# A kernel with a recorded issue order: warm-up in three parts, first tile first on both queues, stores in groups of 6, 6 and 2, and a new order

## The chip, the cores and the metric

One core of a Trainium2 chip runs the whole kernel. The metric is device time in microseconds (us) of one launch; three runs of the kernel before gave 243.06, 243.61 and 245.81 us, so their median is 243.61 us. The engines are TensorE (PE for matmuls, PEld for its weight loads), VectorE (DVE), ScalarE (ACT), GpSimd (POOL) and SyncE (SP), which issues nearly all transfers. A trailing q (SPq, ACTq) marks an engine's instruction queue where it issues transfers or waits.

## What is computed

The reference adds three things over a sequence of 2048 rows of 640 channels: the input x, a long convolution branch A, and a gated MLP branch B. Both branches read the normalised xn.

```python
x = A_q
xn = _layernorm(x, axis=-1)
# A: k shifted by a 4-tap filter, times v; convolved with ssm_k over the sequence by FFT; times xn
kv = k_shift * v
y = irfft(rfft(kv_pad) * rfft(ssm_k_pad))[:S] + kv * ssm_D
A = xn * y
# B: gated MLP with 1728 hidden columns
g = xn @ w_gate ; u = xn @ w_up
B = (sigmoid(g) * u) @ w_down
out = x + A + B
```

## The kernel before, in words

**The MLP.** The 2048 rows lie in `acc` as 16 tiles of 128 rows. Four tiles make a group `tr` (0 to 3). A group is normalised (`rec_norm`), transposed (`rec_tp`: group 0 on TensorE, the others by a transposing transfer from the scratch `xnd`) and multiplied with the gate and up weights in 14 column blocks `fc` (`rec_first` for the first two blocks of group 0, line 753; `rec_fc` for the rest, line 774: five matmuls of 128x512 for each half). ScalarE makes the sigmoid (736), VectorE the product `hT` (738, 733, 727). `rec_down` (790) multiplies `hT` with `w_down`, seven matmuls to a half, and VectorE adds the result into `acc` (801). The last tile, 15, is done in column pieces of 320, 240 and 80.

**The convolution.** Its FFT is written as matmuls in ten steps `idx`. For each: VectorE makes the shifted product `kvt` (484 to 491), TensorE does stage 1 (510) and stage 2 (530), the results go from PSUM to SBUF through casts (329, 330, 332), two transfers swap the halves of S into P (550), VectorE multiplies the spectra (552, 559, 562, 564; the last writes the part called q), TensorE does stage 3 (578), and the results go to V. When all ten are done, stage 4 (610) makes the output in six pieces `c4_0` to `c4_5` of 3, 3, 3, 3, 2 and 2 tiles; VectorE multiplies each with xn (618) and adds it to `acc` (619).

**The start.** Group 0 has to be loaded, normalised and transposed before the first useful matmul. `load_x` (367) loads tile 0 by itself (four transfers of 32 partitions) and tiles 1 to 3 together (four more); two of each four go through SP's queue and two through ACT's. Statistics of tiles 0 to 2 are VectorE's (`rec_stat`, 640 and 642), those of tile 3 ScalarE's (647 to 653); `rec_fast` (658, 660) makes the reciprocal of the deviation by a square root on ScalarE and a reciprocal on VectorE; line 684 normalises; line 706 transposes. Meanwhile TensorE runs matmuls whose result nobody reads (`warm`, line 819): nine at once and one more later.

**The order.** Every piece of work is recorded as an operation with a number, the tiles that it reads and writes and the engines that may run it. `ORDER` is the list of those numbers in which all are emitted, so it sets the order on each engine and each queue; `ON_DVE` names the operations that go to VectorE where ScalarE could do them too (mostly casts out of PSUM). `few`, `pri`, `size` and the durations in the operations are numbers for the planner that once made the list; in the emitted program they are nothing. The names in an operation's `r` list are the same: they bind the planner. The waits in the program come from the tiles that the emitted instructions really touch.

**Transfers.** Each transfer signals its landing on one of eight semaphores, taken in turn over both queues. An instruction that issues a transfer waits until the transfer that used the same semaphore before it has landed.

**The end.** `store` writes finished tiles: tiles 0 to 7 (four transfers of 32 partitions), 8 to 13 (four), 14 (four), and tile 15 in three column pieces (line 627, one transfer each). All are issued by SP.

Of the kernel before, what the change touches and what calls it, by code (L numbers as in the profile page):

```python
# [15 lines left out]
ACT = mybir.ActivationFunctionType  # L16
# [6 lines left out]
NQ = S // P  # L23
# [21 lines left out]
def _dft_tables():  # L45
# [31 lines left out]


ORDER = [
# [38 lines left out]
]  # L118
ON_DVE = [
    98, 102, 104, 139, 140, 142, 147, 148, 195, 248, 380, 397, 424, 445, 446, 470, 480, 486, 498, 504, 605  # L120
]


# [94 lines left out]
def kernel(  # L218
# [38 lines left out]
    acc = cst.tile([P, NQ, DM], BF16, name="acc")  # L257
# [35 lines left out]
    plan = _Plan(SLOTS, ("c", "xq"))  # L293
# [42 lines left out]
    def dma(fn, nd, run, q="SP", few=0.0, **kw):  # L336
        few = few or (1.4 if nd <= 64 and run > 1000 else 1.0)
        plan.op({q: (0.48 + nd / 8000.0, lambda: fn(nc.sync if q == "SP" else nc.scalar))},
                size=1.05 * few * nd * (10.6 + run / 23.8) / 16e3 + 0.03, nd=nd, **kw)
# [25 lines left out]

    def load_x(q, m0, m1, eng, pri):
        dma(lambda e: e.dma_start(acc[32 * q:32 * q + 32, m0:m1, :], xq4[q][:, m0:m1, :]), 32, 1280 * (m1 - m0), q=eng,
            few=1.0 if m0 == 0 else 1.2 if m0 == 1 else 2.4, w=[("acc", m, q) for m in range(m0, m1)], pri=pri)

    def weight(tr, n):  # L370
        tr = 0 if tr == 1 else tr
# [251 lines left out]
    def store(m0, m1, pri, d0=0, d1=DM):  # L623
        key = [("acc", m, x) for m in range(m0, m1) for x in range(4)] if d1 - d0 == DM else (
            [("fin", m, (d0 > 0) + (d0 > 320)) for m in range(m0, m1)] + [("cv", m) for m in range(m0, m1)])
        if m0 >= PRM["ML"]:
            dma(lambda e: e.dma_start(oq4[:, :, m0:m1, d0:d1], acc[:, m0:m1, d0:d1]), 128,
                2 * (d1 - d0) * (m1 - m0), few=3.0, r=key, w=[("out", m0, d0)], pri=pri)
            return
        for q in range(4):  # L630
            dma(lambda e, q=q: e.dma_start(oq4[q][:, m0:m1, d0:d1], acc[32 * q:32 * q + 32, m0:m1, d0:d1]), 32,
                2 * (d1 - d0) * (m1 - m0), few=1.5 if m1 - m0 > 2 else 1.0, r=key, w=[("out", m0, d0, q)], pri=pri)

    MEAN, VAR, RST, TMP, EPS = range(5)

    def rec_stat(m, pri):
        b = f"bs{m}"
        ak = [("acc", m, q) for q in range(4)]
        for s2 in range(2):
            dve(320, 1, lambda s2=s2: nc.vector.bn_stats(tl[b][:, 6 * s2:6 * s2 + 6], acc[:, m, s2 * 320:(s2 + 1) * 320]),  # L640
                r=ak, w=[(b, s2)], alloc=[(b, "bs")] if s2 == 0 else (), pri=pri)
        dve(8, 1, lambda: nc.vector.bn_aggr(st[:, 0:2, m], tl[b].rearrange("p (a c) -> p a c", a=2)),
            r=[(b, 0), (b, 1)], w=[("mv", m)], pri=pri)

# [162 lines left out]
    FIX = -1e6  # L807
# [9 lines left out]
    def warm(n, w=512):  # L817
        for _ in range(n):
            nc.tensor.matmul(tl["wps"][:, 0, 0:w], lhsT=tl["warm"][:, 0:P], rhs=tl["warm"][:, 0:w], start=True, stop=True)
# [26 lines left out]
    rec_fast(3, FIX + 50, 1.0 / DM)  # L846
    rec_norm(0, FIX + 5, True)
    rec_tp(0, FIX, True)
    plan.op({"PE": (0.43, lambda: warm(1))}, r=[("warm",), ("xn0", 0)], w=[("wps", 1)], pri=FIX + 0.5)
    for m0, m1, k in ((4, 8, "LS1"), (8, NQ, "LNS")):  # L850
        if m0 == 4:
            for m in range(m0, m1):
# [31 lines left out]
    for tr in range(4):  # L884
# [5 lines left out]
        if tr < 3:  # L890
            rec_tp(tr + 1, gt())
        rec_down(tr, tr == 3)
    store(0, 8, 240.0)
    store(8, 14, 242.0)
    store(14, 15, 246.0)
    store(15, 16, 247.0, d1=320)
    store(15, 16, 248.0, d0=320, d1=560)
# [32 lines left out]
```

## Time and profile before

| what | value |
|---|---|
| median of three runs | 243.61 us |
| the profiled execution | 244.61 us |
| its span, first to last instruction | 242.8 us |
| TensorE busy with matmuls | 230.0 us (95%) |
| VectorE busy | 195.3 us (80%) |
| ScalarE busy | 153.4 us (63%) |
| HBM read, written | 30.74 MB, 5.24 MB |

The profile is one execution. Its page gives busy time per engine, the span in 40 slices, the transfer queues, the chain of work that ended last, and groups of equal instructions. The views asked of the trace beside the page are the timeline (start, length, engine, source line, written and read tiles, count, and in brackets the idle time before it and what ended it), windows (busy time of each engine in a stretch, with the granted TensorE clock, where 1.00 is full speed), waits, and one source line's durations.

### The profile page before, as it was taken

Reading aid. Unit: us, or ns where it says so; the run is one execution under the profiler, and the core shown is the slowest. Engines: PE = TensorE matmul, PEld = TensorE weight load, DVE = VectorE, ACT = ScalarE, POOL = GpSimd, SP = SyncE. Lnnn points to the kernel's source line nnn. Section 1 sums busy time; section 2 is a strip of 40 time slices with the busy share of each in tenths; the row PEclk is TensorE's granted clock in tenths of the full one; section 3 lists DMA queues with packets and bytes.
Section 4 is the critical chain, followed back from the end, with each engine's and each line's share of the span. In section 5 each row is a group of like instructions: output and inputs, shape, how many; then the busy total and the mean of one; then the engine's idle time right before and its main releaser. Section 6 shows DMA issues by size and latency. Waiting matters only on the chain. (4 is left out here: it accounts for less than half of the span.)

```text
span 242.8 us, 8236 instructions
## 1 busy us (share of the span) xinstructions
PE 230.0 (95%) x3649; PEld 139.3 (57%) x3676; DVE 195.3 (80%) x278; ACT 153.4 (63%) x216; POOL 0.7 (0%) x6
## 2 busy tenths in 40 slices
PE   6699999999999999999999999999999999989891
PEld 1564455775444567675555554777765655456671
DVE  3724577297889898999898999999899499878961
ACT  2713235004799999789988999777689863443320
POOL 1000000000000000000000000000000000000000
PEclk9799999999999999999999999999999999999998
DMA  6999959799988599999997979584443896120591
GB/s 185 313 241 318 160 156 201 200 194 253 158 147 144 135 139 165 219 239 129 237 189 181 287 169 262 122 239 123 121 103 108 222 307 197 55 86 3 153 284 55
DMA packets 92599, 43.72 MB, mean 180 GB/s; under 512 B 69716, under 2 KB 88980, under 8 KB 92308
## 3 DMA queue, kind: packets, MB, share of 16 engines
q1 hardware_dynamic: 92372, 42.87, 76.9%
q8 instruction: 28, 0.46, 0.8%
q10 hardware_dynamic: 192, 0.33, 0.4%
q14 instruction: 7, 0.06, 0.1%
HBM read 30.74 MB, written 5.24 MB: 148 GB/s over the span
## 5 line engine op out<-in xcount | busy, mean ns | idle before, releaser
L774 PE MATMUL g<-xnT,w 128*128 128x512 bf16 x358 | 85.9, 379 | 1.6 <-issue 0.6
L790 PE MATMUL g<-wd,hT 128*128 128x320 bf16 (+2 forms) x462 | 64.5, 295 | 0.7 <-DVE acc L801 0.7
L774 PEld LDWEIGHTS <-w 128*128 128x128 bf16 x380 | 35.3, 98 | 39.1 <-issue 0.8
L790 PEld LDWEIGHTS <-hT 128*128 128x128 bf16 x462 | 43.1, 98 | 16.9 <-issue 0.6
L736 ACT ACTIVATE sig<-g 128x512 bf16<-128x512 f32 x44 | 26.5, 603 | 32.5 <-PE g L774 30.2
L738 DVE TENSOR_TENSOR hT<-sig,g 128x512 bf16<-128x512 bf16 x44 | 30.2, 687 | 20.2 <-PE g L774 17.4
L329 ACT CAST S<-c 128x1024 bf16<-128x1024 f32 (+2 forms) x39 | 37.5, 999 | 10.6 <-PE c L610 5.4
L774 PE MATMUL g<-xnT,VV 128*128 128x512 bf16 x135 | 31.4, 379 | 0.3
L484 DVE TENSOR_TENSOR P<-kt,sT 128x2048 bf16<-128x2048 bf16 x20 | 24.4, 1222 | 0.2
L332 ACT ACTIVATE T<-c 128x1024 bf16<-128x1024 f32 x20 | 19.8, 1027 | 5.4 <-PE c L510 5.4
L801 DVE TENSOR_TENSOR acc<-g,acc 128x320 bf16<-128x320 f32 (+2 forms) x33 | 15.7, 477 | 8.8 <-PE g L790 8.6
L530 PEld LDWEIGHTS <-Mt 64*128 64x128 f16 x1280 | 19.7, 95 | 5.0 <-issue 4.6
L774 PEld LDWEIGHTS <-VV 128*128 128x128 bf16 x140 | 13.4, 98 | 15.6 <-issue 0.2
L329 ACT CAST T<-c 128x1024 bf16<-128x1024 f32 (+1 forms) x20 | 19.6, 1021 | 4.2 <-PE c L610 3.5
L530 PE MATMUL c<-T,Mt 64*128 64x64 bf16 x1280 | 22.0, 190 | 0.0
L329 ACT CAST VV<-c 128x1024 bf16<-128x1024 f32 x18 | 17.9, 1018 | 4.0 <-PE c L578 3.9
L552 DVE TENSOR_TENSOR P<-S,P 128x2048 bf16<-128x2048 bf16 x10 | 12.2, 1219 | 0.6 <-DMA P<-S 0.6
L564 DVE TENSOR_TENSOR S<-P 64x2048 bf16<-64x2048 bf16 x10 | 12.2, 1223 | 0.3
L562 DVE TENSOR_TENSOR S<-S 64x2048 bf16<-64x2048 bf16 x10 | 12.2, 1221 | 0.3
L559 DVE TENSOR_TENSOR S<-S 128x2048 bf16<-128x2048 bf16 x10 | 12.2, 1223 | 0.2
L488 DVE TENSOR_TENSOR P<-P,P 128x2048 bf16<-128x2048 bf16 x10 | 12.2, 1221 | 0.2
L491 DVE TENSOR_TENSOR kvt<-P,vt 128x1024 bf16<-128x1024 bf16 x10 | 11.6, 1158 | 0.0
(73 smaller groups left out, 173.5 us busy)
## 6 DMA issues: line engine op xcount, KB each, us to landing
P<-S SPq DMA_DIRECT2D x20, 256.0 KB, 5.3
w<-in_B_w_gate_dram SPq DMA_DIRECT2D x7, 640.0 KB, 6.7
w<-in_B_w_up_dram SPq DMA_DIRECT2D x7, 640.0 KB, 5.6
kt<-in_A_k_dram SPq DMA_DIRECT2D x8, 320.0 KB, 8.3
xnd<-VV SPq DMA_DIRECT2D x4, 640.0 KB, 4.4
vt<-in_A_v_dram SPq DMA_DIRECT2D x8, 320.0 KB, 7.7
VV<-in_A_ssm_k_dram SPq DMA_DIRECT2D x16, 96.0 KB, 4.6
wd<-in_B_w_down_dram SPq DMA_DIRECT2D x3, 480.0 KB, 4.2
```

The source lines that it names most:

```text
L329: fa = lambda: nc.scalar.copy(out=out_fn(), in_=in_fn())
L332: fa = lambda: nc.scalar.activation(out_fn(), in_fn(), ACT.Copy, scale=scale)
L484: dve(2048, 2, lambda: nc.vector.tensor_tensor(tl[c].rearrange("p i (n c) -> p i n c", c=CJ), two(t), sh(t), ALU.mult), r=kr + [("s",)], w ...
L488: dve(2048, 2, lambda: nc.vector.tensor_tensor(tl[a][:], tl[a][:], tl[b][:], ALU.add), r=[(b,)], w=[(a,)], pri=pri)
L530: nc.tensor.matmul(tl[c][:, b, 64 * kk:64 * kk + 64], lhsT=Mb[rows, (k + 16 * b) % 32, 64 - 64 * r:192 - 64 * r], rhs=tl[T][rows, 2 * k + ...
L552: dve(n, 2, lambda: nc.vector.tensor_tensor(Q(), X(), Q(), ALU.mult), r=[(Z, "h", 0), (Z, "h", 1)], w=[(Z, 0)], pri=pri)
L559: dve(n, 2, lambda: nc.vector.tensor_tensor(X(), X(), H(), ALU.mult), r=[(Z, 0)] + sr, w=[(S_, "p")], pri=pri + 0.01)
L736: act(512, lambda: nc.scalar.activation(tl[sg][:], pv(0), ACT.Sigmoid), r=[pk(0)], w=[(sg,)], alloc=[(sg, "sig")], pri=pri - 2000)
L738: dve(512, 1, lambda: nc.vector.tensor_tensor(hT[:, fc, :], tl[sg][:], pv(1), ALU.mult), r=[pk(1), (sg,)], w=[(hk, fc)], pri=pri - 2000)
L774: nc.tensor.matmul(tl[c][:], lhsT=w()[:, k, o:o + P], rhs=tl[X][:, k, :], start=(k == 0), stop=(k == NC - 1))
L790: nc.tensor.matmul(tl[pd[i]][:, 0:d1 - d0], lhsT=hT[:, fc, t4 * P:(t4 + 1) * P], rhs=wd[:, fc, d0:d1], start=(fc == 0), stop=(fc == NFC - 1))
L801: dve(d1 - d0, 1, lambda i=i, m=m, pd=pd, d0=d0, d1=d1: nc.vector.tensor_tensor(acc[:, m, d0:d1], tl[pd[i]][:, 0:d1 - d0], acc[:, m, d0:d1 ...
```

## The change

- `ORDER` and `ON_DVE` are new lists. `ORDER` has 884 numbers where it had 879, since five operations are added; `ON_DVE` has 23 where it had 21.
- Warm-up: nine matmuls as before, then two recorded as reading the statistics of tile 0, then one recorded as reading the first transpose and the statistics of tile 1. Before, the second part was one matmul recorded as reading the normalised tile 0.
- Tile 0: in the new order the first two `load_x` transfers of SP's queue and of ACT's are those of tile 0. Before, SP's second one was of tiles 1 to 3, and its third of tile 0. The statistics of tile 1 are recorded as reading the reciprocal of tile 0, so VectorE has tile 0's reciprocal and normalisation ahead of tile 1's statistics; the copy of tile 0's transpose comes right behind them. On TensorE the order is: eleven warm-up matmuls, transposes of tile 0, one warm-up matmul, transposes of tile 1, the products of tiles 0 and 1, transposes of tiles 3 and 2.
- Stores: tiles 0 to 5, 6 to 11, 12 and 13, then 14, then 15 in the same three pieces. The four transfers of tile 14 are issued by ACT, the others by SP.
- `load_x` has another planner number for tiles 1 to 3.

In the new order the last transfers stand so on the two queues (four transfers q0 to q3 to a store; in brackets the transfer whose landing is waited for through the shared semaphore, where it is a late one):

```text
ACT: tile 14 q0, q1, q2, q3
SP:  tiles 0-5 q0, q1; load of xn; tiles 0-5 q2, q3; tiles 6-11 q0, q1; tiles 12-13 q0, q1, q2;
     tiles 12-13 q3 [tile 14 q0]; tiles 6-11 q2 [tile 14 q1]; tiles 6-11 q3;
     tile 15 320 columns [tile 14 q2]; tile 15 80 columns [tile 14 q3]; tile 15 240 columns
```

TensorE's last groups become: tile 14, tile 15's 320 columns, the first half of its 240 columns, its 80 columns, the second half of the 240. Before they were tile 14, 240, 320 and 80 columns.

```diff
 ORDER = [
-    1, 0, 5, 8, 10, 4, 7, 6, 12, 3, 11, 9, 72, 73, 74, 77, 78, 75, 76, 79, 87, 88, 92, 97, 13, 15, 80, 81, 93, 99, 89,
+    1, 0, 5, 7, 6, 8, 4, 9, 11, 10, 12, 3, 72, 73, 74, 105, 75, 76, 92, 97, 77, 78, 79, 98, 87, 88, 80, 81, 93, 82,
...
 ON_DVE = [
-    98, 102, 104, 139, 140, 142, 147, 148, 195, 248, 380, 397, 424, 445, 446, 470, 480, 486, 498, 504, 605
+    98, 102, 104, 138, 144, 145, 148, 150, 151, 181, 194, 198, 326, 422, 439, 441, 444, 447, 465, 469, 486, 498, 516
 ]
...
-            few=1.0 if m0 == 0 else 1.2 if m0 == 1 else 2.4, w=[("acc", m, q) for m in range(m0, m1)], pri=pri)
+            few=1.0 if m0 == 0 else 2.0 if m0 == 1 else 2.4, w=[("acc", m, q) for m in range(m0, m1)], pri=pri)
...
-                2 * (d1 - d0) * (m1 - m0), few=1.5 if m1 - m0 > 2 else 1.0, r=key, w=[("out", m0, d0, q)], pri=pri)
+                2 * (d1 - d0) * (m1 - m0), few=1.5 if m1 - m0 > 2 else 1.0, q="ACT" if m0 == NQ - 2 else "SP",
+                r=key, w=[("out", m0, d0, q)], pri=pri)
...
-                r=ak, w=[(b, s2)], alloc=[(b, "bs")] if s2 == 0 else (), pri=pri)
+                r=ak + ([("rs", 0)] if m == 1 else []), w=[(b, s2)], alloc=[(b, "bs")] if s2 == 0 else (), pri=pri)
...
-    plan.op({"PE": (0.43, lambda: warm(1))}, r=[("warm",), ("xn0", 0)], w=[("wps", 1)], pri=FIX + 0.5)
+    plan.op({"PE": (0.86, lambda: warm(2))}, r=[("warm",), ("mv", 0)], w=[("wps", 1)], pri=FIX + 0.5)
+    plan.op({"PE": (0.43, lambda: warm(1))}, r=[("warm",), ("pst0_0", 0), ("mv", 1)], w=[("wps", 2)], pri=FIX + 0.5)
...
-    store(0, 8, 240.0)
-    store(8, 14, 242.0)
+    store(0, 6, 238.0)
+    store(6, 12, 240.0)
+    store(12, 14, 242.0)
     store(14, 15, 246.0)
     store(15, 16, 247.0, d1=320)
```

74 rows, old and new, of the table ORDER are left out of this document.

## The prediction

> **What bounds the kernel now.** I read the page first: the busy table, the slices, the chain.
>
> ```profile
> span 242.8 us, 8236 instructions
> ...
> PE 230.0 (95%) x3649; PEld 139.3 (57%) x3676; DVE 195.3 (80%) x278; ACT 153.4 (63%) x216; POOL 0.7 (0%) x6
> ...
> PEclk9799999999999999999999999999999999999998
> ...
> PE 4%; DVE 0%; issue 0%
> ```
>
> TensorE is busy for 95% of the span, 12.8 us of which it is idle. Everything else can only matter where TensorE waits, or after its last matmul. The chain covers only 4% of the span, so it says little, and I went on to windows and the timeline. The columns of the windows are: stretch, its length, busy time and instructions of PE, PEld, DVE, ACT and POOL, granted clock, DMA share, GB/s.
>
> ```profile
> 2.18:5.59 3.41, 3.06 (x8) 0.78 (x6) 1.10 (x3) 1.51 (x2) 0.00 (x0) 1.00 0.95 264
> 5.59:9.00 3.41, 0.90 (x11) 0.68 (x12) 2.55 (x9) 2.50 (x8) 0.00 (x0) 1.00 1.03 315
> 9.00:12.41 3.41, 3.39 (x32) 3.06 (x30) 1.86 (x7) 2.27 (x3) 0.00 (x0) 0.50 1.10 308
> 65.00:191.00 126.00, 124.58 (x2344) 77.17 (x2360) 118.33 (x148) 109.48 (x151) 0.00 (x0) 1.00 0.81 173
> 195.00:211.00 16.00, 15.65 (x102) 7.56 (x97) 14.76 (x17) 7.81 (x12) 0.00 (x0) 1.00 0.63 196
> ```
>
> TensorE leaves 0.90 busy in 5.59 to 9.00, and the next window of 3.41 us is granted half the clock. From 65 to 191 TensorE is busy for 124.58 of 126.00 us and VectorE for 118.33 (94%): the middle is TensorE's, with VectorE close behind. So three places can move the time: the start, the points where VectorE hands over to TensorE, and the end.
>
> **The change, part by part.** Times are those of the profiled execution (244.61 us, 1.00 above the median of 243.61); I carry differences over to the median.
>
> *Warm-up and tile 0.* Rows of the start, for TensorE, VectorE, ScalarE and SP in turn:
>
> ```profile
> 1.22 4.02 PE L819 MATMUL c<-sig 128*128 128x512 bf16 x9 [1.22 <-DVE sig L808]
> 7.86 0.45 PE L706 MATMUL g<-VV 128*128 128x128 bf16 x5 [2.62 <-DVE VV L684]
> 8.56 0.45 PE L706 MATMUL g<-VV 128*128 128x128 bf16 x5 [0.24 <-DVE VV L684]
> 9.35 3.28 PE L753 MATMUL c<-xnT,VV 128*128 128x128 bf16 x30
> ...
> 4.20 0.89 DVE L640 BATCH_NORM_STATS2 bs<-acc 128x6 f32<-128x320 bf16 x2 [2.43 <-DMA acc<-in_A_q_dram]
> 6.36 0.89 DVE L640 BATCH_NORM_STATS2 bs<-acc 128x6 f32<-128x320 bf16 x2 [1.03 <-DMA acc<-in_A_q_dram]
> 7.16 0.15 DVE L660 RECIPROCAL st<-st 128x1 f32<-128x1 f32 x1
> 7.41 0.39 DVE L684 TENSOR_SCALAR VV<-acc,st 128x640 bf16<-128x640 bf16 x1
> 7.86 0.16 DVE L660 RECIPROCAL st<-st 128x1 f32<-128x1 f32 x1
> 10.50 0.45 DVE L684 TENSOR_SCALAR VV<-acc,st 128x640 bf16<-128x640 bf16 x1
> ...
> 5.36 0.29 ACT L658 ACTIVATE st<-st 128x1 f32<-128x1 f32 x1 [1.48 <-DVE st L642]
> 7.53 0.29 ACT L658 ACTIVATE st<-st 128x1 f32<-128x1 f32 x1 [0.16 <-DVE st L642]
> ...
> 0.73 1.80 SPq L367 DMA_DIRECT2D acc<-in_A_q_dram  x4
> ```
>
> Before, VectorE waits 1.03 us for tile 1's data and does its statistics (6.36 on) ahead of tile 0's reciprocal, although the square root for tile 0 is there at 5.36 + 0.29 = 5.65. With the new order the reciprocal (0.15) and the normalisation (0.39) run inside that wait, and tile 0's transposes can start near 6.3 instead of 7.86. With one SP issue (1.80 / 4 = 0.45) fewer ahead of tile 0's second piece, its statistics may come up to 0.45 earlier still. But the first useful matmuls (L753, 9.35) need tile 1's transposes (8.56) too, and tile 1 hangs on its data, its statistics at 6.36 and the square root that ends at 7.53 + 0.29 = 7.82; the next VectorE step starts at 7.86, right behind it. None of that moves. Tile 1's own transposes stay at 8.56; only tile 2's normalisation (10.50) gains, since 0.54 us of VectorE work left the stretch, and I take -0.2 us from it. Bounds: 0 if tile 1's data come later (its SP transfers now issue behind tile 0's), -0.45 if all that tile 0 gains is passed on.
>
> The two added warm-up matmuls cost 4.02 / 9 = 0.45 each and end by 1.22 + 11 x 0.447 = 6.1, ahead of the transposes; the third part (0.45) lies between tile 0's and tile 1's transposes, where TensorE is idle. They cost nothing. The word "gated" holds for the planner alone: a name in an operation's list of reads binds the order, the matmul itself touches only `sig` and a PSUM tile, so nothing on the chip makes it wait. Its place in the order still fills the idle stretch: with the same windows, 5.59 to 9.00 would hold about 0.5 + 0.45 + 0.45 + 0.45 = 1.9 us of work instead of 0.90.
>
> *The clock.* The half-speed window holds 30 L753 matmuls in 3.28 us, and at full speed they take half, so it costs up to 1.7 us; about 0.3 of it would be lost anyway, to tiles 2 and 3. Does 1.9 us of work prevent it? No row says; the gap before tile 1 shrinks from 2.62 to about 1.4 us. The bounds are 0 and -1.4. I take 0, since a window that is half empty stands nearer to the one quoted (0.90) than to a full one (3.06). [...]
>
> *New lists.* By count, `ON_DVE` sends two more results to VectorE. The dearest such row:
>
> ```profile
> L330 DVE CAST S<-c 128x1024 bf16<-128x1024 f32 (+1 forms) x5 | 6.1, 1214 | 0.0
> ```
>
> Two of them are 2.4 us of VectorE work (the types differ: it may be less), against 126.00 - 118.33 = 7.7 us idle in the middle. Through most of the kernel the convolution's steps stand within some 3 us of their old places on TensorE, so I cost this at nothing: the idle 7.7 us cover it. Without that cover it costs 2.4. TensorE's work, and the number of its changes between the small convolution matmuls and the gate and up matmuls, are the same.
>
> The one handover that visibly loses its margin is the last convolution step:
>
> ```profile
> 195.41 9.74 PE L774 MATMUL g<-xnT,w 128*128 128x512 bf16 x44 [0.16 <-issue]
> 210.73 1.07 PE L578 MATMUL c<-At,S 128*128 128x128 f16 x16
> 217.01 0.78 PE L610 MATMUL c<-VV,kt 32*32 32x160 bf16 x66 [0.63 <-issue]
> 226.27 0.97 PE L790 MATMUL g<-wd,hT 128*128 128x320 bf16 x6 [0.66 <-DVE acc L801]
> ...
> 196.55 0.69 DVE L738 TENSOR_TENSOR hT<-sig,g 128x512 bf16<-128x512 bf16 x1 [0.40 <-PE g L774]
> 209.45 1.22 DVE L564 TENSOR_TENSOR S<-P 64x2048 bf16<-64x2048 bf16 x1
> ```
>
> VectorE's last product ends at 210.67 and stage 3 starts at 210.73: 0.06 of margin. Between that step's stage 2 and stage 3 the old order has 45 and 20 gate and up matmuls, the new one 35 and 20: ten fewer, 10 x 9.74 / 44 = 2.2 us less cover. VectorE's list for the stretch loses two hT products (0.69 each), 1.4 us. So TensorE waits 2.2 - 1.4 - 0.06 = 0.75 us. Against that the 0.63 at 217.01 may go, since the sharing of casts behind it changes: bounds 0 and -0.63, and I take -0.3. The 0.66 at 226.27 stays. Interior: +0.4, between -1.3 (both waits go and the handover holds) and +2.9 (the 2.4 above on top).
>
> *Stores.* The rows of the end: TensorE, VectorE, SP, the store's line by itself, and the DMA view (us from issue to landing last).
>
> ```profile
> 230.70 6.87 PE L790 MATMUL g<-wd,hT 128*128 128x320 bf16 x63
> ...
> 234.09 0.49 DVE L801 TENSOR_TENSOR acc<-g,acc 128x320 bf16<-128x320 f32 x1
> ...
> 233.57 3.28 SPq L631 DMA_DIRECT2D out_dram<-acc  x5
> 236.95 0.64 SPq L627 DMA_DIRECT2D out_dram<-acc  x1
> 237.63 0.47 SPq L631 DMA_DIRECT2D out_dram<-acc  x1
> 238.21 1.22 SPq L627 DMA_DIRECT2D out_dram<-acc  x2
> ...
> L631 SPq DMA_DIRECT2D out_dram<-acc x12: 314/494/1142, 225.8 to 237.6; - x12
> ...
> out_dram<-acc SPq DMA_DIRECT2D x4, 40.0 KB, 2.4
> ```
>
> The last matmul ends at 230.70 + 6.87 = 237.57; SP's last issue ends at 238.21 + 1.22 = 239.43; the span ends 3.37 later, at 242.8. What ends the kernel is SP's row of issues, not VectorE. The change gives tile 14's four issues to ACT, which alone would free 4 x 0.49 of SP. But the queue as it now stands has the last transfer of tiles 12 and 13 wait for the landing of tile 14's first one, through the shared semaphore. Tile 14 is finished at 234.09 + 0.49 = 234.58; its 40 KB land 2.4 later: 237.0. Only then does SP go on, with six issues: three of L631 at 3.28 / 5 = 0.66, and those of tile 15 at 0.64 and 1.22 for two, with gaps of 0.05 between: 3.9 us. The last issue ends near 240.9 instead of 239.43, so **the tail is 1.5 us longer**. Behind that wait stand two 240 KB stores of tiles 6 to 11 that could have gone long before. The wider last add (240 columns instead of 80) hides behind this queue. Bounds: -0.6 if the wait ends before SP gets there (SP three or four issues shorter, then VectorE's wider add is last), +2.7 if tile 14 lands later or the two large stores delay tile 15's by their own landing.
>
> The sum: -0.2 + 0.4 + 1.5 = +1.7. Profiled: 246.3; median: 245.3.
>
> **The rivals.**
> - *The clock is held.* As the sum, with the start at -1.6 instead of -0.2: 243.61 - 1.6 + 0.4 + 1.5 = 243.9. For it speaks the fuller window, against it that over 1 us of idleness is left before tile 1. Chance 0.22.
> - *VectorE becomes the bound* (the other side: slower). Place: the casts and products ahead of a stage 3; price: the two casts, 2.4 us, on top: 247.7. It decides as soon as the products reach TensorE with no margin, as they do at 210.73 (0.06) and as 94% in the middle lets one fear; against it stand the 7.7 us of idle time. Chance 0.20.
> - *The store queue does not hold.* Tail -0.6: 243.61 - 0.2 + 0.4 - 0.6 = 243.2. For it: ACT takes four issues. Against it: the semaphore's turn, read off the new order. With the clock held as well: 241.8. [...] Chance 0.10.
> - *The change does nothing measurable at the start*, since the gates are not in the program: that is part of the forecast.
>
> **How the numbers follow.** Forecast 245.3, chance 0.48 (its own range 244.2 to 246.6: start bounds, a handover up to 0.7 worse, a tail from +0.6 to +2.4). Clock held 0.22 (243.0 to 244.8), VectorE 0.20 (246.3 to 248.5), queue free 0.10 (241.8 to 243.8). One per cent, about what a measurement of this kernel tells from no change, is 241.2 to 246.05. Slower: nearly all of VectorE's case and a fifth of the forecast's, 0.30. Faster: a part of the queue's case, 0.03. Same: 0.67. Range 242.8 to 247.7: it leaves out the upper part of VectorE's case (0.10) and the lower part of the queue's and the clock's (0.07).
>
> **What would show it.** Tile 0's transposes near 6.3 and tile 1's still near 8.56: the start is right; a granted clock of 0.50 in a window after 9 is the forecast, none is the first rival. An idle time of about 0.75 before the last L578: the handover; several waits on VectorE there, or VectorE above 98% in the middle, the second rival. SP idle before a store of tiles 12 and 13 until about 0.6 us before the last matmul's end, and 6.7 us from the last matmul to the span's end instead of 5.2: the tail. Wrong it is if TensorE shows new waits elsewhere, on transfers of weights above all.

## The result and the profile after

The changed kernel takes 245.50 us (median of 21 runs, 244.86 to 247.04), the kernel before 244.06 (21 runs, 242.43 to 245.81): a ratio of 1.0062, 95% interval 1.0041 to 1.0084. The forecast was 245.3, "same" within 1%. The profiled execution took 246.64 us, so it lies 1.1 above the median; that of before lay 0.55 above its own. Between the two profiled executions there are 2.0 us, and the lines below explain those.

First the page of the changed kernel: span and busy times.

```profile
span 244.9 us, 8247 instructions
...
PE 229.6 (94%) x3649; PEld 138.1 (56%) x3678; DVE 197.4 (81%) x280; ACT 151.7 (62%) x214; POOL 0.7 (0%) x6
```

TensorE has as much to do as before. The windows of the same stretches (columns as before: stretch, length, PE, PEld, DVE, ACT, POOL, clock, DMA share, GB/s), and one more at the end:

```profile
5.59:9.00 3.41, 1.51 (x20) 1.04 (x19) 2.85 (x9) 2.60 (x8) 0.00 (x0) 1.00 1.06 308
9.00:12.41 3.41, 3.41 (x58) 3.14 (x57) 2.17 (x9) 2.00 (x3) 0.00 (x0) 1.00 1.05 322
65.00:191.00 126.00, 124.58 (x2329) 76.49 (x2346) 117.25 (x147) 108.65 (x151) 0.00 (x0) 1.00 0.79 170
210.00:230.00 20.00, 19.49 (x609) 12.77 (x611) 17.30 (x21) 9.76 (x12) 0.00 (x0) 1.00 0.27 70
```

The same last stretch in the kernel before:

```profile
210.00:230.00 20.00, 18.64 (x545) 11.96 (x544) 17.41 (x20) 8.23 (x11) 0.00 (x0) 1.00 0.23 57
```

Three things are to be seen. The window from 9.00 on is at full clock and holds 58 matmuls instead of 32. The middle is the same to the last digit for TensorE (124.58), and VectorE is not fuller (117.25 instead of 118.33). From 210 to 230 TensorE is idle for 0.51 us instead of 1.36. All this is in favour of the change. The losses stand in the timeline of TensorE, with two rows of ScalarE among them (start, length, engine, line, operation, in brackets the idle time before it and what ended it):

```profile
1.22 4.73 PE L820 MATMUL c<-sig 128*128 128x512 bf16 x11 [1.22 <-DVE sig L809]
5.78 0.44 PE L707 MATMUL g<-VV 128*128 128x128 bf16 x5
8.35 0.45 PE L707 MATMUL g<-VV 128*128 128x128 bf16 x5 [1.90 <-DVE VV L685]
8.63 1.84 PE L754 MATMUL c<-xnT,VV 128*128 128x128 bf16 x30
10.45 0.73 PE L707 MATMUL g<-VV 128*128 128x128 bf16 x10
...
14.62 0.71 PE L754 MATMUL c<-xnT,VV 128*128 128x256 bf16 x5 [0.69 <-ACT sig L737]
...
33.55 0.71 PE L754 MATMUL c<-xnT,VV 128*128 128x256 bf16 x5 [0.95 <-ACT sig L737]
...
13.98 0.60 ACT L737 ACTIVATE sig<-c 128x512 bf16<-128x512 f32 x1 [2.96 <-PE c L754]
32.90 0.60 ACT L737 ACTIVATE sig<-c 128x512 bf16<-128x512 f32 x1 [0.76 <-DVE hT L728]
...
210.20 1.07 PE L578 MATMUL c<-At,S 128*128 128x128 f16 x16 [0.37 <-DVE S L564]
216.12 0.76 PE L610 MATMUL c<-VV,kt 32*32 32x160 bf16 x64 [0.20 <-issue]
230.15 6.89 PE L791 MATMUL g<-wd,hT 128*128 128x320 bf16 x63
```

Two waits for a sigmoid, 0.69 and 0.95, are new: the matmuls start at 14.62 and 33.55, right behind the sigmoids' ends at 14.58 and 33.50. Even so the last matmul ends at 230.15 + 6.89 = 237.04, 0.53 earlier than before (237.57). The whole loss lies behind it: from there to the span's end 7.86 us pass instead of 5.23. The end, on ScalarE's and SP's queues (SP's last issues one by one), with SP's waits in total, tile 14's transfers in the DMA view (KB each, us from issue to landing), and the landing times of all transfers of line 631:

```profile
234.35 1.75 ACTq L631 DMA_DIRECT2D out_dram<-acc  x4
...
235.91 0.32 SPq L631 DMA_DIRECT2D out_dram<-acc  x1
...
236.36 0.33 SPq L631 DMA_DIRECT2D out_dram<-acc  x1
...
236.73 2.04 SPq L631 DMA_DIRECT2D out_dram<-acc  x1
...
238.87 1.94 SPq L627 DMA_DIRECT2D out_dram<-acc  x3
...
SPq L631 <- DMA out_dram<-acc: 5.0, 4, 2.4
...
out_dram<-acc ACTq DMA_DIRECT2D x4, 40.0 KB, 1.5
...
DMA to landing us min/median/max: 1.5/3.6/4.9
```

SP waits up to 2.4 us for the landing of a store; it goes on at 235.91, 1.56 after ScalarE issued the first transfer of tile 14, which lands in 1.5. One of the two large issues behind it then takes 2.04 us by itself, and the last issue ends at 240.81.

### The profile page after: what moved, and what is told of

Its sections match the earlier page's. It is cut to its first block, busy times and chain, and to the rows that moved or that the text cites. A ratio compares the mean times of both kernels' runs of the same rounds, so it can differ in the third digit from the quotient of the medians.

```text
span 244.9 us, 8247 instructions
## 1 busy us (share of the span) xinstructions
PE 229.6 (94%) x3649; PEld 138.1 (56%) x3678; DVE 197.4 (81%) x280; ACT 151.7 (62%) x214; POOL 0.7 (0%) x6
## 4 chain that ended last, share of the span: by engine, by line
PE 85%; DVE 7%; issue 2%; DMA 2%; ACT 1%; ACTq 1%; DVEq 0%
PE g L775 40%; PE g L791 26%; PE c L530 8%; PE c L578 4%; PE c L510 3%; PE c L610 2%; PE c L754 2%; DMA acc<-in_A_q_dram 2%; DVE S L559 1%; DVE S L562 1%; DVE P L552 1%; DVE S L564 1%; DVE hT L728 1%; DVE hT L739 1%; ACTq L367 1%
## 5 line engine op out<-in xcount | busy, mean ns | idle before, releaser
L329 ACT CAST S<-c 128x1024 bf16<-128x1024 f32 (+2 forms) x41 | 39.3, 1001 | 10.4 <-PE c L530 5.4
L332 ACT ACTIVATE T<-c 128x1024 bf16<-128x1024 f32 x19 | 19.2, 1029 | 3.3 <-PE c L510 3.3
L329 ACT CAST T<-c 128x1024 bf16<-128x1024 f32 (+1 forms) x19 | 18.8, 1015 | 3.7 <-PE c L610 2.1
L329 ACT CAST VV<-c 128x1024 bf16<-128x1024 f32 x17 | 16.8, 1017 | 2.4 <-PE c L578 2.2
```

What stands on the lines that cost most here:

```text
L329: fa = lambda: nc.scalar.copy(out=out_fn(), in_=in_fn())
L332: fa = lambda: nc.scalar.activation(out_fn(), in_fn(), ACT.Copy, scale=scale)
```

## The experiments

Each run of the table is given beside the kernel before on the same chip. "Tail" is the time from the last matmul's end to the span's end in the profile, "30 products" the time of the first 30 matmuls of the products (1.84 at full clock). In the run "changed, sigmoids behind" a part of the matmul records is missing at the end, and the last add of VectorE, which starts within 0.05 of the last matmul's end in the others, gives its tail.

| kernel | ratio to before (95%) | tail, us | 30 products, us |
|---|---|---|---|
| before | 1 | 5.2 | 3.28 |
| changed | 1.0062 (1.0041 to 1.0084) | 7.9 | 1.84 |
| changed, old stores | 0.9972 (0.9947 to 0.9998) | 4.9 | 1.84 |
| changed, large stores earlier | 1.0004 (0.9972 to 1.0036) | 5.7 | 1.84 |
| before, new stores | 1.0097 (1.0070 to 1.0124) | 7.5 | 2.68 |
| changed, sigmoids behind | 0.9978 (0.9949 to 1.0007) | 7.2 | 1.84 |
| changed, tile 14 on SP | 0.9997 (0.9967 to 1.0027) | 5.2 | 1.84 |
| old stores and sigmoids behind | 0.9912 (0.9877 to 0.9946) | 5.0 | 3.20 |
| the same, again | 0.9930 (0.9888 to 0.9972) | 4.9 | 1.84 |
| before, new head | 1.0004 (0.9976 to 1.0032) | 4.9 | 1.84 |
| before, 11 warm-ups at the start | 0.9980 (0.9951 to 1.0009) | 4.6 | 3.36 |
| both undone, 9 warm-ups | 1.0024 (0.9995 to 1.0053) | 5.0 | 3.41 |
| both undone, old head | 1.0208 (1.0169 to 1.0246) | 4.9 | 3.41 |
| both undone, tile 14 in one transfer | 0.9942 (0.9913 to 0.9971) | 5.4 | 3.22 |

**The stores put back.**

```diff
-q="ACT" if m0 == NQ - 2 else "SP",
+q="SP",
...
-    store(0, 6, 238.0)
-    store(6, 12, 240.0)
-    store(12, 14, 242.0)
+    store(0, 8, 240.0)
+    store(8, 14, 242.0)
```

> The changed kernel with the stores of the kernel before (tiles 0 to 7, 8 to 13, 14, all on SP, tile 14 ahead of tile 15), all else as changed. In the changed kernel 7.9 us pass from the last matmul to the span's end, before 5.2. Theory (the SP queue is held by the landing of tile 14, with two large stores behind it): back to 5.2, so 245.5 - 2.6 = 242.9 us. Rival (the new order of tile 15's pieces on TensorE, with 240 columns last, makes the tail long): 7 us or more stay, 244.9 or more.

Its last matmuls and SP's last issues:

```profile
228.82 7.16 PE L792 MATMUL g<-wd,hT 128*128 128x320 bf16 x63
...
235.66 1.94 SPq L628 DMA_DIRECT2D out_dram<-acc  x3
```

The last issue ends 1.6 us after the last matmul (237.60 and 235.98) instead of 3.8, and the tail is 4.9 us. By the ratios 0.9% comes back, 2.2 us. The order of tile 15's pieces, which was kept, is not the cause.

**The stores alone, in the kernel before.** The same edit the other way round, with the new places of the stores in the order.

> The kernel before with only the new stores (6, 6, 2; tile 14 on ACT's queue; the new places in the order). Theory (the stores alone make the tail): 5.2 grows to 7.9 us, so 2.6 slower than before, 246.7 beside 244.1. Rival (the rest of the new order is needed for the loss): within 0.8 of before.

1.0097, 2.4 us, and a tail of 7.5: the stores alone make the loss, in the old order of the rest as in the new one.

**What stands behind the wait.** In the changed order the third and fourth transfer of tiles 6 to 11 (numbers 871 and 872) are moved right behind the first two:

```diff
-869, 870, 851, 875, 876, ...
+869, 870, 871, 872, 851, 875, 876, ...
```

> The changed kernel with the third and fourth transfer of tiles 6 to 11 issued right behind the first two; the wait of SP for the landing of tile 14 stays, but behind it stand two 80 KB stores of tiles 12 and 13 and the three of tile 15 instead of two 240 KB ones more. Theory (what stands behind the wait is the price): SP goes on at about 1.1 us before the last matmul's end, five short issues take 3.0 us, the end comes 3.4 later: 5.3 us from the last matmul, 245.5 - 2.5 = 243.0 us. Rival (the wait alone is the price, whatever stands behind it): 7 us or more, 244.9 or more.

```profile
228.70 6.89 PE L793 MATMUL g<-wd,hT 128*128 128x320 bf16 x63
...
236.11 1.94 SPq L629 DMA_DIRECT2D out_dram<-acc  x3
```

The last issue ends at 238.05, 2.5 us after the last matmul (235.59) instead of 3.8; the tail is 5.7. That is near the 5.3 expected of the theory and far from the 7 of the rival; the time, 244.25, lies between their figures (243.0 and 244.9) and nearer to the rival's: by the ratios 1.4 us come back, where the old stores brought 2.2. The wait stays (2.3 us in this profile), and the larger part of its price goes with the two large stores.

**Tile 14 on SP, groups kept.**

```diff
-q="ACT" if m0 == NQ - 2 else "SP",
+q="SP",
```

> The changed kernel with tile 14's four transfers issued by SP like all others; groups of 6, 6 and 2 and all places in the order kept. Theory (the shared semaphore between ACT's tile 14 and SP's queue is the price): SP no longer waits for a landing; seven issues stand behind tile 14's last add, 4 us, so 5.4 us from the last matmul's end instead of 7.9, 245.5 - 2.4 = 243.1 us. Rival (the groups of 6, 6 and 2 and their late places are the price, on whatever queue): 7 us or more, 244.8 or more.

The tail is 5.2 us, near the 5.4 of the theory; by the ratios 0.65% comes back, 1.6 us instead of 2.4. In this profile SP issues all stores without a wait for the landing of another. A price of the groups of 6, 6 and 2 by themselves does not show (0.9997 beside 0.9972 with the old stores; the intervals overlap). It is the second queue, through the semaphore that it shares with SP's, that costs, and it costs mostly because large stores stand behind the wait.

**The sigmoids behind the up half.** Two places in the order: 164 and 162 are the sigmoids of blocks 1 and 0, 161 and 159 the matmuls of their up halves.

```diff
-160, 164, 522, 161, 521, ... 162, 159,
+160, 522, 161, 164, 521, ... 159, 162,
```

> The changed kernel with two places swapped in the order: the sigmoids of the first two column blocks stand behind the block's up half on TensorE, not between its gate half and its up half. In the changed kernel TensorE waits for them, 0.69 us at 14.6 and 0.95 at 33.6. Theory (the matmul waits for the whole PSUM tile that the sigmoid reads): both waits go, 245.5 - 1.6 = 243.9 us, and the last matmul ends 1.6 us earlier. Rival (TensorE would wait there for something else, a transfer or a buffer): 245.5 unchanged, the waits under another name.

The row that had 0.95 us of idle time ahead of it, and all that TensorE waits for in this kernel:

```profile
31.60 0.71 PE L756 MATMUL c<-xnT,VV 128*128 128x256 bf16 x5
...
PE g L709 <- DVE VV L687: 2.4, 2, 2.1
PE c L822 <- DVE sig L811: 1.2, 1, 1.2
PE c L580 <- DVE S L566: 0.3, 1, 0.3
```

No wait for a sigmoid is left, and the time falls from 1.0062 to 0.9978, 2.0 us (1.6 expected). Gate and up half of a block are two halves of one PSUM tile (`tl[c][:, 0]` and `tl[c][:, 1]`): the sigmoid reads the one, the matmul writes the other, and still the matmul waits (0.69 and 0.95 us). In the old order the sigmoid of a block comes only after both halves, and TensorE has no wait for a sigmoid there. Whether the program keeps the two apart because it counts by whole tiles, or the chip needs it, these runs don't separate.

**Both undone.** The old stores and the sigmoids behind the up half together, in two separate runs of the same kernel.

> The changed kernel with the sigmoids of the first two blocks behind their up halves and with the stores of the kernel before. By themselves these gave -1.9 and -1.9 beside the changed kernel. Theory (two separate losses at the two ends of the kernel): they add up, 245.5 - 3.8 = 241.7 us, 1 per cent under the kernel before. Rival (TensorE's gain at the start is given back at a later wait once the tail is short): 243 or more.

> The kernel with the sigmoids behind and the old stores once more, as the base for the three beside it: 0.991 of the kernel before, 242.2 beside 244.4.

0.9912 and 0.9930 of the kernel before: 0.7 to 0.9% faster than before and some 1.4% faster than the changed kernel. The two losses add up. What is left of the change is a gain of about 2 us.

**Where that gain is from.** First the new head alone, ahead of the old order (the changed order's first 62 entries, then the old order without them, with the changed warm-ups and `rec_stat`):

> The kernel before with only the head of the new order (its first 62 entries: transfers of tile 0 first, the new VectorE order, eleven and one warm-up matmuls, transposes and first products of group 0), then the old order; old stores. The prediction's step: the head gives -0.2 at the same clock, 243.9 beside 244.1. Rival (the added warm-ups keep the clock up): -1.4 to -1.6, 242.6, and no window at half clock behind 9 us.

```profile
7.93 0.45 PE L708 MATMUL g<-VV 128*128 128x128 bf16 x5 [1.55 <-DVE VV L686]
8.22 1.84 PE L755 MATMUL c<-xnT,VV 128*128 128x128 bf16 x30
...
13.14 1.25 PE L776 MATMUL g<-xnT,VV 128*128 128x512 bf16 x4 [0.97 <-DMA VV<-in_B_w_gate_dram]
15.47 5.57 PE L776 MATMUL g<-xnT,VV 128*128 128x512 bf16 x25 [1.08 <-DMA VV<-in_B_w_up_dram]
```

The clock is kept in this profile, tile 1's transposes come 0.6 earlier, and nothing is won: TensorE arrives at the gate and up weights 2.05 us before they have landed. In this kernel a faster start pays only as far as the loads behind it are early enough (0.97 and 1.08 us of wait for them here). The reverse, the old head ahead of the new rest, goes worse:

> The same with the head of the kernel before (its first 65 entries, its two warm-ups, tile 1's statistics ahead of tile 0's reciprocal) and then the new order. In the old order the new head gave nothing, since TensorE then waited 2.1 us for weights. Theory (the new rest is what lets the new head count): 1 to 1.7 us slower than with the new head, 243.5. Rival (the head is worth nothing there either, and the 2 us come from the new order of the rest, from its last 50 us above all): within 0.4 us.

```profile
17.91 1.25 PE L775 MATMUL g<-xnT,VV 128*128 128x512 bf16 x4 [3.16 <-DMA VV<-in_B_w_gate_dram]
```

It is 2.1% slower than before, far more than either expectation. Both mixtures move the early loads against their users, so neither gives the worth of the head by itself. Then the warm-ups, in two ways. Eleven instead of nine at the start of the kernel before:

```diff
-lambda: warm(9)
+lambda: warm(11)
```

> The kernel before with eleven warm-up matmuls at the start instead of nine (one more behind the first transposes, as it was), nothing else. Rival of the prediction (more warm-up keeps the clock): the first useful matmuls at full speed, -1.4, 242.7. Prediction (a window that is half idle still halves the clock): within 0.3 of 244.1, and the half-speed stretch is there.

Half speed still (3.36 for the 30 products), 0.9980, and the interval includes 1. And the other way, both losses undone but without the added warm-ups:

```diff
-lambda: warm(2)
+lambda: None
...
-lambda: warm(1))}, r=[("warm",), ("pst0_0", 0), ("mv", 1)]
+lambda: None)}, r=[("warm",), ("pst0_0", 0), ("mv", 1)]
```

> The same without the added warm-ups: nine matmuls at the start, none behind tile 0's transposes. Theory (the warm-ups keep the clock up at the first products, worth 1.4): half-speed products again in most executions, 0.8 to 1.4 us slower than with them. Rival (tile 0's and tile 1's earlier transposes are what counts, the warm-ups nothing): within 0.4 us.

```profile
8.54 3.41 PE L755 MATMUL c<-xnT,VV 128*128 128x128 bf16 x30
11.74 1.27 PE L708 MATMUL g<-VV 128*128 128x128 bf16 x10
12.81 1.71 PE L755 MATMUL c<-xnT,VV 128*128 128x128 bf16 x20
```

1.0024 instead of 0.993: 2.3 us, more than the 1.4 that the theory asked for, since the half speed goes on behind the 30 products (ten transposes take 1.27, where the changed kernel took 0.73). In this profile the clock rises for the first time at 13.70. This is the whole gain that was left. As far as these runs tell, the added warm-ups, together with the earlier tile 0 whose transposes stand among them, are what the change earns.

**Tile 14 in one transfer.** On top of both undone, `ML=15` becomes `ML=14`: one transfer of 128 partitions instead of four of 32.

> The same as the first, with tile 14 stored by one transfer of 128 partitions instead of four of 32. Theory (SP's row of issues ends the kernel): three issues of 0.45 fewer, and the last issue can follow the last add at once instead of 0.65 later: -0.6 us. Rival (the landing of the last transfers sets the end, not the issues): no change.

```profile
232.58 0.82 DVE L619 TENSOR_TENSOR vt<-vt 128x1280 bf16<-128x1280 bf16 x1 [2.25 <-DMA vt<-xnd]
...
234.92 2.10 PE L792 MATMUL g<-wd,hT 128*128 128x240 bf16 x28 [1.63 <-DVE acc L803]
```

No gain (0.9942 beside 0.9912 and 0.9930). The issues are fewer, but in this kernel VectorE waits 2.25 us for the last load of xn, which lies in SP's queue between the large stores, and TensorE waits for VectorE. The same two waits are there in the second run of both undone, 1.39 and 0.77 us. Issuing that load ahead of the stores was not tried.

## Why the prediction held, and where it did not

The time was right by luck: four errors cancel. On the profiled executions the sum should have been -0.2 + 0.4 + 1.5 = +1.7 and was +2.1:

*The start: -0.2 forecast, -2.0 measured.* Up to the transposes of tiles 2 and 3 both kernels do the same useful matmuls, and these transposes start at 10.45 instead of 12.46. Two rows of the kernel before:

```profile
8.85 0.48 PE L819 MATMUL c<-sig 128*128 128x512 bf16 x1
...
12.46 0.72 PE L706 MATMUL g<-VV 128*128 128x128 bf16 x10
```

Tile 0's and tile 1's transposes came at 5.78 and 8.35 (6.3 and 8.56 forecast), so the chain up to there was read rightly. Two steps failed. The smaller one is that nothing but tile 2 would gain: the single warm-up matmul that stood between tile 1's transposes and the products (8.85, 0.48 us) now stands ahead of tile 1's transposes. So the products start 0.72 earlier (8.63 instead of 9.35), and only 0.21 of that is tile 1's. The larger one is "I take 0" for the clock: the window from 9.00 on was at full clock, and from the first of the 30 products to the transposes behind them 1.82 us pass instead of 3.11, which is 1.29 less. That was the first rival, given 0.22. In the profiles of kernels with the new head and all twelve warm-ups the products ran at 1.84 in seven of nine; with the old head or nine warm-ups they took 2.68 to 3.41 in all five. My reason, that a window of 1.9 us of work stands nearer to 0.90 than to 3.06, was an estimate, and no run shows how much work keeps the clock; the window held even less than that, 1.51 us, and the idle stretch before tile 1 was 1.90 us instead of 1.4.

The traces tell more when the windows are laid at their own clock steps. In every profile the warm-up matmuls run at half speed at first (0.43 us from one to the next; at full clock, in the changed kernel at 25.96, five matmuls of 512 columns take 1.08 to the start of the next, 0.22 each), and the record of the clock in the trace begins where it rises: in the changed kernel at 5.67, inside the eleventh warm-up matmul. In the first run of both undone it rises at 5.32 and drops at 8.73 for 3.41 us. The 3.41 us from the rise to the drop and the 3.41 at half clock, for the first run of both undone, and then two stretches of the same length behind the rise in the changed kernel:

```profile
5.32:8.73 3.41, 1.62 (x17) 0.84 (x16) 3.23 (x10) 2.45 (x8) 0.00 (x0) 1.00 1.11 328
8.73:12.14 3.41, 3.41 (x36) 3.41 (x33) 1.40 (x6) 2.15 (x3) 0.00 (x0) 0.50 1.08 323
...
5.67:9.08 3.41, 1.51 (x20) 1.12 (x20) 2.85 (x10) 2.68 (x8) 0.00 (x0) 1.00 1.07 314
9.08:12.49 3.41, 3.41 (x56) 3.10 (x55) 2.09 (x9) 1.92 (x3) 0.00 (x0) 1.00 1.04 318
```

The very same kernel, both undone, shows 3.20 us for the 30 products in this profile and 1.84 in that of its second run. The length of the longest gap does not decide: the stretch with the drop behind it has 1.51 us of idle time in one piece, the one without has 1.90. Nor does the busy time of the stretch, 1.62 us ahead of the drop and 1.51 without one, as far as it can be read, since the profile models the end of each matmul. What decides is not shown by these fourteen profiles.

The warm-ups go with the time of the rise. With nine at the start the clock had risen by 5.6 us in two profiles, and in the other two (the kernels that the table shows with 3.41) it rose only at 13.7 and 13.1; with eleven it had risen by 7.3 us in all ten. The twelfth and the earlier tile 0 then add work behind the rise: from 5.59 to 9.00 TensorE is busy for 0.90 us in the kernel before, for 1.33 with eleven warm-ups in the old order and for 1.51 in the changed kernel.

*The last convolution steps: +0.75 - 0.3 forecast, -0.7 measured.* The handover lost its margin as forecast, but half as much: 0.37 us of wait instead of 0.75. The wait of 0.63 shrank to 0.20 (-0.3 forecast). The one of 0.66, which I let stand without looking at what is ahead of it in the new order, is gone: 0.37 - 0.43 - 0.66.

*The new lists: "I cost this at nothing", +1.64 measured.* (With the start at -2.0 and the last steps at -0.7 this would put the last matmul 1.1 earlier; it is 0.53 earlier, so that some 0.5 us more are lost at places that these rows don't show.) The sum of VectorE's work was the wrong place to look; the second rival, VectorE as the bound, did not come. The price came from two pairs of operations whose order on two engines was turned round, each a sigmoid ahead of the up half of its own PSUM tile. The order of instructions, which was there to be read, shows it.

*The tail: +1.5 forecast, +2.6 measured.* The mechanism was right, and the experiments tell it from its rivals: the wait for tile 14's landing through the shared semaphore, and the large stores behind it. Its size was off. SP went on earlier than I had it (1.13 us before the last matmul's end instead of 0.6, since tile 14's 40 KB landed in 1.5 us and not in 2.4), but the six issues took 4.90 us instead of 3.9, because one of the 240 KB stores took 2.04 to issue; and the span ends 4.1 after the last issue instead of 3.37, with tile 15's stores behind others that need up to 4.9 us to land. ScalarE's queue took over four issues, 1.75 us in all; in the changed kernel even that was lost again in the wait.

That the gates of the warm-up are not in the program was right: the eleven matmuls stand back to back at 1.22. The place in the order was enough.

## What to carry to other kernels

When transfers move to a second queue, look which later transfer of the first queue shares a completion semaphore with them, and what stands behind that one; keep large stores ahead of it (here SP waited up to 2.4 us, and 1.4 us came back when the two 240 KB stores went ahead). When an order is remade, go through the pairs of operations that touch one PSUM tile on two engines before weighing the sums of work: a read put between two matmuls of a tile can be a wait (0.69 and 0.95 us here), however idle the reading engine is (ScalarE had been idle for 2.96 and 0.76 us). And a change can hide a gain and two losses under a difference of half a per cent: undoing its parts one at a time gave a kernel 0.7 to 0.9% faster than the one before.

## What was not expected of the hardware

- The granted clock in the profile reads 1.00 in stretches where the matmuls show half speed: in the run with nine warm-ups and the new head this window reads 1.00, while 30 products take 3.41 us. The trace of that run has its first record of the clock at 13.70, where it rises, and the view shows 1.00 for the time ahead of it. The duration of equal matmuls is the safer sign.

```profile
9.00:12.41 3.41, 3.41 (x35) 3.41 (x34) 0.94 (x4) 1.96 (x3) 0.00 (x0) 1.00 0.97 293
```

- An issue of a store on SP (line 631) took 0.35 us in the median of the changed kernel and 0.49 before, but 2.04 for a 240 KB store right behind another one; what holds it the runs don't tell.
- Three matmuls of 512 columns whose result nobody reads are worth 2.3 us of 243 in this kernel (1.0024, 0.9995 to 1.0053, without them and 0.9930, 0.9888 to 0.9972, with them).
